# Another order of the opening table in a fused attention and MLP kernel on one core

## The chip, the core and the metric

The kernel runs on one core of a Trainium2 chip. Its engines work side by side, each on its own list of instructions in order: TensorE (PE in the profile, with the loading of weights shown apart as PEld), VectorE (DVE), ScalarE (ACT), GpSimd (POOL) and SyncE (SP). SyncE does nothing here but issue transfers. An instruction that needs another engine's result, or data from a transfer, waits on a semaphore, and everything behind it on its own engine waits with it. The metric is the device time of the whole program in microseconds; the time before is a median of 347.26 us over five runs (347.07 to 348.0).

## The reference, cut to what matters

```python
# B, H, S, D = 8, 8, 576, 64; d_model = 512, d_ff = 2048
scores = matmul(q, k.T) / sqrt(D)
cum    = cumsum(log(clip(f, 0.0001, 1.0)), axis=-1)
scores = where(causal, -1e9, scores + cum[:, :, :, None] - cum[:, :, None, :])
attn   = softmax(scores)
x      = matmul(attn, v)              # heads side by side: 4608 x 512
h      = x @ w_in                     # 4608 x 2048
out    = gelu_tanh(h) @ w_out         # 4608 x 512
```

The decay of a query divides out of the softmax. So the kernel needs only the exponentials of the scores and, for each key, a weight exp(-cum): it multiplies the values by that weight, and sums the weights themselves through the same probabilities for the denominator.

## The kernel before

The 64 pairs of batch and head are taken in 16 quads of four heads. Quad i belongs to batch i // 2. For one quad the work is as follows.

- Its keys and queries come as bf16 by GpSimd's transfers (load_one, L154) into one of two buffers each (k_c, q_c); VectorE transposes them (L160) into kT and qT.
- Scores (L215) are computed on TensorE with a key block as the stationary operand, into one of two PSUM tiles (psS), and ScalarE takes their exponential (L223) into pt. Quads 0 and 1 are cut into four rounds (split_rounds), others into three.
- Diagonal blocks of pt are masked, either on GpSimd by an affine_select (mask, L229) or on VectorE by a product with a triangle (mask_by_product, L258).
- The values of the batch, v_nat, arrive by SyncE's transfers (load_v, L131), one for each block of 128 keys. They are multiplied by the key weights into vw (make_vw, L177), on GpSimd or VectorE.
- The denominators (L269 or L283, then VectorE's L302, L304, L306) and two value products (L269 or L283, then VectorE's L314) give the quad's part of xT. Quads 0 and 1 do this in two parts, of 256 and of 320 queries; the products of the parts use one of two PSUM tiles (psM).
- When both quads of a batch are done, the MLP's input product (L325, or L342 for the first chunk of 512 tokens in halves of 256) with the GELU on ScalarE, and its output product (L363) follow. The output product is a generator, so that it is run in small pieces between other work on TensorE.

The order of the first part of the program is written out in a table, FRONT, which run() walks word by word. The scheduler is set to manual, so the place of a word in the table is the place of its instructions on each engine's list. A word is a name, its arguments, and after an @ an earlier transfer that it has to wait for (a gate). The words that the change and the prediction touch:

- LK.i, LQ.i: issue the load of quad i's keys or queries (GpSimd). LU.t: issue the load of block t of batch 0's values (SyncE). LV.b.h: the same for half the heads of batch b, five blocks. WI.c, WO.c: issue a quarter of w_in or w_out (GpSimd).
- TK.i, TQ.i: the transposes (VectorE). SB: the running sums of log f on GpSimd. CW: the key weights (TensorE, ScalarE). W: their copy as bf16 (VectorE). TR: the triangles. Z: five memsets on GpSimd.
- S.i.r: the scores of a round for four heads; H.i.r.g: for the heads of pair g alone.
- M.i.r and m.i.r: the mask on GpSimd and on VectorE. VW.i.part and vw.i.part: make_vw on GpSimd and on VectorE. CL: a small copy in vw.
- D.i.part, V.i.x.part: denominators and value products. J.half.g: a piece of the first input product. I.c.p: a piece of the second. F.c.n and f.c.n: n pieces of output product c.
- B.n.cols: n matmuls on a tile of zeros, whose result nobody reads.

GpSimd's transfers all share the software queue (q0), SyncE's the hardware queue (q1). A value block arrives in packets of 256 bytes, keys and queries in 2304 bytes, w_in in 2048, w_out in 1024.

Two gates matter most. In the table before, the load of value block 0 waits for quad 1's queries, and the first load of w_in waits for that value block:

```python
LU.1@LK.0 B.3.256                                   # SETUP
WO.0@LK.0 LU.0@LQ.1 SB TK.0 TQ.0 CW S.0.0 TR W LU.2 # FRONT, first words
WI.0@LU.0 H.1.1.0 M.1.0 D.1.0
```

After the table come the chunks 2 to 8 in a loop, which the change doesn't touch.

Of the kernel before, what the change touches and what calls it, by code (L numbers as in the profile page):

```python
# [16 lines left out]
def kernel(  # L17
# [10 lines left out]
    nc = tc.nc  # L28

    B, H, S, D = q.shape  # L30
    BH = B * H
# [35 lines left out]
    LOW, HIGH = NT, NT - 1  # L67

    SETUP = """
        LU.1@LK.0 B.3.256  # L70
    """

    FRONT = """
        WO.0@LK.0 LU.0@LQ.1 SB TK.0 TQ.0 CW S.0.0 TR W LU.2 B.2.128 B.2.384 B.4.256 Z M.0.0 TK.1 S.0.2 B.2.384 TQ.1 LU.3@LQ.1
        D.0.0 H.1.0.0 B.1.256 vw.1.0 H.1.0.1 vw.0.0 H.0.1.1 B.4.128 H.0.1.0 V.0.1.0 V.0.0.0 WI.0@LU.0 H.1.1.0 M.1.0 D.1.0 V.1.1.0 WI.1@WO.0 LU.4 m.0.1 H.0.3.1
        B.3.256 H.0.3.0 V.1.0.0 m.0.3.2 LK.3 vw.0.1 M.0.3.4 LQ.2 H.1.2.1 B.2.256 H.1.2.0 D.0.1 H.1.3.0 H.1.3.1 V.0.1.1 V.0.0.1 H.1.1.1 WI.2@LU.3 vw.1.1 m.1.1
        M.1.3 J.0.1 D.1.1 V.1.0.1 WI.3@LU.2 V.1.1.1 WO.2@LU.4 WO.1 LK.2 WO.3 LV.1.1@LK.2 J.0.0 J.1.1 TQ.2 J.1.0 J.1.2 J.0.3 J.0.2 LQ.3 LV.1.0@LK.2
        J.1.3 TK.2 F.0.6 S.2.0 LK.4 F.0.12 TQ.3 S.2.2 TK.3 F.0.10 S.2.1 TK.4 M.2.0 vw.3 M.2.2 F.0.5 F.0.5 LQ.5 S.3.0 M.2.1
        f.0.4 LQ.4 D.2 VW.2 f.0.2 LV.3.0@LK.4 CL.2 S.3.1 f.0.6 LK.5 LV.2.1@LV.3.0 V.2.0 M.3.1 S.3.2 f.0.6 TQ.4 m.3.2 CL.3 LV.2.0@LK.4 V.2.1
        S.4.1 F.0.5 H.4.2.1 M.3.0 D.3 f.0.1 H.4.0.1 H.4.0.0 LK.6 V.3.1 v.3.0 f.0.2 TQ.5 H.4.2.0 VW.5 I.1.1 I.1.6 I.1.0 LQ.7 vw.4  # L80
        I.1.2 m.4.0 TK.6 I.1.7 LQ.6 I.1.3 CL.5 I.1.5 I.1.4 F.1.8 TK.5 CL.4 LK.7 S.5.0 f.1.7 TQ.6 M.4.1 M.4.2.3 M.4.2.2 D.4
        S.5.1 LV.3.1 m.5.1 F.1.10 S.5.2 V.4.0 f.1.5 m.5.0 V.4.1 S.6.0 M.5.2 f.1.3 D.5 VW.6 f.1.4 S.6.1 V.5.1 M.6.1 f.1.5 V.5.0
        LQ.8 M.6.0 LK.8 S.6.2 CL.6 M.6.2 F.1.14
    """

    singles = ctx.enter_context(tc.tile_pool(name="singles", bufs=1))
# [6 lines left out]
    def many(n, shape, dtype, name):  # L93
        return [singles.tile(shape, dtype, name=f"{name}{i}") for i in range(n)]
# [11 lines left out]
    vw = many(2, [128, NT + 1, 4, D], BF16, "vw")  # L106
# [6 lines left out]
    logfT = singles.tile([128, NT * BH], FP32, name="logfT")  # L113
    before = singles.tile([128, (NT - 1) * BH], FP32, name="before")
# [296 lines left out]
            nc.vector.tensor_copy(m, utri_f32)  # L411
        nc.vector.tensor_copy(causal[1][64:128, 0:64], utri_f32[0:64, 0:64])

    def sums_before():
        nc.gpsimd.tensor_copy(before[:, 0:BH], logfT[:, 0:BH])
        for t in range(1, NT - 1):
            nc.gpsimd.tensor_add(before[:, t * BH:(t + 1) * BH],
                                 before[:, (t - 1) * BH:t * BH],
                                 logfT[:, t * BH:(t + 1) * BH])

# [28 lines left out]
    def load_values(b, half):  # L449
# [2 lines left out]
    ops = {  # L452
        "W": cast_w,
        "CW": make_w,
        "SB": sums_before,
        "Z": zeros,
        "TR": triangles,
        "S": lambda i, r: scores(i, r),
# [111 lines left out]
```

## Time and profile before

| quantity | value |
| --- | --- |
| median of five runs | 347.26 us |
| time of the profiled execution | 347.95 us |
| its span in the trace | 346.2 us |
| TensorE busy | 331.6 us |
| ScalarE busy | 191.1 us |
| VectorE busy | 134.9 us |
| GpSimd busy | 97.0 us |
| mean granted TensorE clock | 0.985 |

The profile is of one execution; its time is 1.7 us over its span, which lies around the recorded instructions, and 0.7 us over the median. TensorE is busy nearly throughout, so time is to be looked for in the places where it idles or where its clock is lowered. The page has the busy shares in 40 slices, and the trace answers in windows of any length, with the clock that was granted in each.

### The profile page before, as it was taken

The page shows a single profiled execution, that of the slowest core. Times are in us where ns is not written, and L with a number is a line of the kernel's source. Part 1 is how long each engine was busy: PE and PEld are TensorE (multiplying, and loading weights), DVE is VectorE, ACT ScalarE, POOL GpSimd, SP SyncE. Part 2 cuts the span into 40 slices and gives each one's busy share as a digit, 9 for nine tenths or more (in the row PEclk, how much of TensorE's full clock was granted, in tenths as well). Part 3 has the DMA queues.
Part 4 walks back from the last instruction along what each step waited for, and adds up shares of the span by engine and source line. Part 5 has one row for each costly group of instructions (what it writes and reads, how often), then busy time and mean ns, then how long its engine had stood idle before and what let it go on. Part 6 is the DMA issues. An engine that isn't in the chain of part 4 may idle for free.

```text
span 346.2 us, 9348 instructions
## 1 busy us (share of the span) xinstructions
PE 331.6 (96%) x4200; PEld 162.9 (47%) x4221; DVE 134.9 (39%) x204; ACT 191.1 (55%) x192; POOL 97.0 (28%) x139
## 2 busy tenths in 40 slices
PE   3879999999899999999999999999999999999996
PEld 2336854544454444444544444444444554444443
DVE  4766127755361534352445145404530360002011
ACT  3746577775666475746664667457655623520510
POOL 7336116233043216420552065104510320000000
PEclk9958999999999999999999999999999999999999
DMA  7998998878015871068105901380100011001002
GB/s 124 216 160 134 181 217 174 184 185 154 3 64 98 173 155 41 34 140 165 63 34 110 195 33 65 80 157 32 63 32 2 32 51 44 0 32 61 30 32 91
DMA packets 51000, 33.26 MB, mean 96 GB/s; under 512 B 38992, under 2 KB 41296, under 8 KB 50960
## 3 DMA queue, kind: packets, MB, share of 16 engines
q0 software_dynamic: 7808, 13.63, 23.8%
q1 hardware_dynamic: 43008, 18.96, 20.5%
q8 instruction: 33, 0.54, 0.7%
q10 hardware_dynamic: 144, 0.07, 0.1%
q14 instruction: 7, 0.06, 0.1%
HBM read 36.85 MB, written 9.44 MB: 134 GB/s over the span
## 4 chain that ended last, share of the span: by engine, by line
PE 90%; DMA 4%; issue 2%; POOL 2%; ACT 1%; DVE 1%; POOLq 0%; DVEq 0%; ACTq 0%
PE pso L363 35%; PE ps_h L325 32%; PE ps_s L215 9%; PE po L283 8%; PE ps_h L342 4%; DMA q_c<-in_q_dram 2%; PE po_m L269 2%; DMA v_nat<-in_v_dram 1%; ACT pt L223 1%; POOL vw L177 1%; DVE vw L177 1%; PE ps_o L283 0%; PE idle_ps L194 0%; POOL pt L229 0%; POOL k_c L154 0%
## 5 line engine op out<-in xcount | busy, mean ns | idle before, releaser
L363 PE MATMUL pso<-w_out_sb,gT 128*32 128x512 bf16 (+2 forms) x1469 | 133.9, 377 | 0.8 <-issue 0.6
L223 ACT ACTIVATE pt<-ps_s 128x1024 bf16<-128x1024 f32 (+2 forms) x100 | 94.3, 991 | 43.2 <-PE ps_s L215 41.4
L325 PE MATMUL ps_h<-xT,w_in_sb 128*128 128x512 bf16 x499 | 112.0, 379 | 0.8 <-issue 0.2
L332 ACT ACTIVATE gT<-ps_h 128x1024 bf16<-128x1024 f32 x64 | 65.5, 1023 | 77.0 <-PE ps_h L325 77.0
L363 PEld LDWEIGHTS <-gT 128*32 128x32 bf16 (+1 forms) x1477 | 56.4, 97 | 56.6 <-issue 2.4
L325 PEld LDWEIGHTS <-w_in_sb 128*128 128x128 bf16 x512 | 49.6, 98 | 61.4 <-issue 2.5
L229 POOL TENSOR_SCALAR_AFFINE_SELECT pt<-pt 128x512 bf16<-128x512 bf16 (+3 forms) x70 | 42.2, 613 | 119.4 <-ACT pt L223 114.9
L368 DVE COPY o_st<-pso 128x512 f32<-128x512 f32 (+2 forms) x37 | 25.0, 676 | 86.0 <-PE pso L363 85.9
L215 PE MATMUL ps_s<-qT,kT 32*128 32x64 bf16 (+5 forms) x896 | 38.1, 269 | 1.5 <-ACT pt L223 1.1
L302 DVE STREAM_TRANSPOSE den<-po 128x576 f32<-128x576 f32 x14 | 11.0, 783 | 53.7 <-PE po L283 53.7
L314 DVE TENSOR_TENSOR xT<-po,rb 128x576 bf16<-128x576 f32 x26 | 19.7, 757 | 29.0 <-PE po L283 28.9
L177 POOL TENSOR_TENSOR vw<-v_nat,wT 128x1280 bf16<-128x1280 f32 x12 | 28.0, 2330 | 10.7 <-DMA v_nat<-in_v_dram 10.7
L215 PEld LDWEIGHTS <-kT 32*128 32x128 bf16 x896 | 17.2, 94 | 25.5 <-issue 20.0
L160 DVE STREAM_TRANSPOSE kT<-k_c 128x576 f32<-128x576 f32 x16 | 19.9, 1246 | 10.2 <-DMA k_c<-in_k_dram 9.2
L283 PE MATMUL po<-pt,vw 128*32 128x64 bf16 (+4 forms) x624 | 22.5, 279 | 0.0
L160 DVE STREAM_TRANSPOSE qT<-q_c 128x576 f32<-128x576 f32 x16 | 19.9, 1242 | 4.7 <-DMA q_c<-in_q_dram 4.7
L154 POOL DMA_DIRECT2D k_c<-in_k_dram x16 | 9.1, 567 | 43.9 <-DVE kT L160 39.5
L283 PEld LDWEIGHTS <-vw 128*32 128x32 bf16 x672 | 14.0, 97 | 12.1 <-issue 4.7
L342 PE MATMUL ps_h<-xT,w_in_sb 128*128 128x256 bf16 x128 | 14.3, 273 | 0.0
L342 PEld LDWEIGHTS <-w_in_sb 128*128 128x128 bf16 x128 | 12.4, 98 | 1.7 <-issue 0.2
L306 DVE STREAM_TRANSPOSE rb<-rec 128x576 f32<-128x576 f32 (+2 forms) x18 | 12.8, 712 | 0.6
L283 PE MATMUL po<-pt,w_bf 128*32 128x512 bf16 (+3 forms) x336 | 12.3, 278 | 0.3 <-POOL pt L229 0.3
(59 smaller groups left out, 114.0 us busy)
## 6 DMA issues: line engine op xcount, KB each, us to landing
out_dram<-o_st SPq DMA_DIRECT2D x35, 256.0 KB, 2.1
v_nat<-in_v_dram SPq DMA_DIRECT2D x20, 256.0 KB, 6.0
k_c<-in_k_dram POOLq DMA_DIRECT2D x16, 288.0 KB, 6.0
q_c<-in_q_dram POOLq DMA_DIRECT2D x16, 288.0 KB, 6.9
v_nat<-in_v_dram SPq DMA_DIRECT2D x29, 128.0 KB, 4.4
w_out_sb<-in_moe_w_out_dram POOLq DMA_DIRECT2D x4, 512.0 KB, 10.3
w_in_sb<-in_moe_w_in_dram POOLq DMA_DIRECT2D x4, 512.0 KB, 7.0
v_nat<-in_v_dram SPq DMA_DIRECT2D x6, 64.0 KB, 4.9
```

Source lines behind the costliest of these rows:

```text
L160: nc.vector.transpose(out=dst.rearrange("p s c -> p (s c)").bitcast(FP32) .rearrange("p (t a) -> p a t", a=S // 32), in_=src.rearrange("p ...
L177: eng.tensor_mul(vw[i % 2][:, t0:t1], vb[:, t0:t1, h0:h0 + 4, :], wT[:, i, t0:t1, :].unsqueeze(3).to_broadcast([128, t1 - t0, 4, D]))
L215: nc.tensor.matmul(tiles[h // 2][:, h % 2, c0:c0 + nq], key_columns(i, key, h, c), qq[32 * h:32 * h + 32, q0:q0 + nq, c], start=(c == 0 an ...
L223: nc.scalar.activation(p[:, 2 * g:2 * g + 2, off:off + n], t[:, :, 0:n], AF.Exp, scale=scale)
L229: nc.gpsimd.affine_select(out=x, in_=x, compare_op=ALU.is_ge, fill=0.0, base=0, pattern=pattern, channel_multiplier=-1)
L283: nc.tensor.matmul(po[r0:r0 + w.shape[-1], 448 + q0:448 + q0 + nq], w, p[:, h, col:col + nq], start=(key in (0, "low")), stop=(key in ("lo ...
L314: nc.vector.tensor_mul(xT[:, 2 * u + x, S * b + s0:S * b + s1], po, rbs[i, part])
L325: nc.tensor.matmul(ph[:, j, :], w_in_sb[:, dt, 128 * ft:128 * ft + 128], xT[:, dt, CH * c:CH * (c + 1)], start=(dt == 0), stop=(dt == N_DT ...
L332: nc.scalar.activation(gT[c % 2][:, 2 * pr:2 * pr + 2, :], ph, AF.Gelu_apprx_tanh)
L342: nc.tensor.matmul(ph[:, j // 2, QA * (j % 2):QA * (j % 2) + QA], w_in_sb[:, dt, 128 * ft:128 * ft + 128], xT[:, dt, n0:n0 + QA], start=(d ...
L363: nc.tensor.matmul(pso[c0:c0 + cols, m0:m1], gT[c % 2][:, ft, 128 * n + c0:128 * n + c0 + cols], w_out_sb[:, ft, m0:m1], start=(ft == 0), ...
L368: nc.vector.tensor_copy(st[:, m0:m1], pso[:, m0:m1])
```

## The change

SETUP is emptied and FRONT gets another order. What differs, by kinds:

- Value loads. Block 4 goes first, after quad 0's keys have landed; blocks 0, 1 and 2 follow with no later gate; block 3 waits for block 4. Before, block 1 went first, block 0 waited for quad 1's queries, and 2, 3 and 4 came behind it.
- w_in and w_out. Only WI.0 keeps its gate; WI.1, WI.2 and WI.3 lose theirs, and WI.3 and WI.2 come right after the mask M.0.1. WO.0 loses its gate. WO.1 to WO.3 are issued together, WO.1 behind value block 3. Half-batch value loads LV.1.1 and LV.1.0 wait for WO.2 and LQ.3 instead of LK.2.
- The first masks of quad 1 (M.1.0) go from GpSimd to VectorE (m.1.0), as do some later ones; M.0.1 and M.1.1 go the other way. make_vw of quad 1's second part and of quads 4 and 5 is on GpSimd, of quads 2, 3 and 6 on VectorE.
- TK.1 and TQ.1 go ahead of W and TR on VectorE, both halves of quad 1's first scores go ahead of D.0.0, and D.0.0's mask M.0.0 goes ahead of the memsets Z on GpSimd.
- Zero matmuls: B.3.128 ahead of S.0.0 (768 columns become 384), 1920 columns (before: 2048) between S.0.0 and S.0.2, 1024 columns (before: 768) behind S.0.2, and one later group, B.3.256, in place of four.
- A new word, sb, would run the sums on VectorE; the table doesn't use it.

```diff
     SETUP = """
-        LU.1@LK.0 B.3.256
+        
     """
     FRONT = """
-        WO.0@LK.0 LU.0@LQ.1 SB TK.0 TQ.0 CW S.0.0 TR W LU.2 B.2.128 B.2.384 B.4.256 Z M.0.0 TK.1 S.0.2 B.2.384 TQ.1 LU.3@LQ.1
-        D.0.0 H.1.0.0 B.1.256 vw.1.0 H.1.0.1 vw.0.0 H.0.1.1 B.4.128 H.0.1.0 V.0.1.0 V.0.0.0 WI.0@LU.0 H.1.1.0 M.1.0 D.1.0 V.1.1.0 WI.1@WO.0 LU.4 m.0.1 H.0.3.1
-        B.3.256 H.0.3.0 V.1.0.0 m.0.3.2 LK.3 vw.0.1 M.0.3.4 LQ.2 H.1.2.1 B.2.256 H.1.2.0 D.0.1 H.1.3.0 H.1.3.1 V.0.1.1 V.0.0.1 H.1.1.1 WI.2@LU.3 vw.1.1 m.1.1
-        M.1.3 J.0.1 D.1.1 V.1.0.1 WI.3@LU.2 V.1.1.1 WO.2@LU.4 WO.1 LK.2 WO.3 LV.1.1@LK.2 J.0.0 J.1.1 TQ.2 J.1.0 J.1.2 J.0.3 J.0.2 LQ.3 LV.1.0@LK.2
+        TK.0 TQ.0 TK.1 B.3.128 LU.4@LK.0 WO.0 SB CW TQ.1 W S.0.0 B.1.128 TR LU.0 B.4.256 M.0.0 B.2.384 S.0.2 B.4.256 H.1.0.1
+        H.1.0.0 D.0.0 H.0.1.1 LU.1 vw.0.0 H.1.1.1 B.3.256 Z m.1.0 vw.1.0 H.0.1.0 LU.2@LK.0 WI.1 V.0.1.0 WI.0@LU.0 M.0.1 D.1.0 LU.3@LU.4 H.1.1.0 WI.3
+        WI.2 V.0.0.0 LK.2 H.0.3.1 V.1.1.0 H.0.3.0 vw.0.1 m.0.3 V.1.0.0 H.1.3.0 H.1.3.1 D.0.1 H.1.2.0 M.1.1 M.1.3 LQ.2 H.1.2.1 V.0.0.1 V.0.1.1 D.1.1
+        J.0.1 VW.1.1 V.1.1.1 WO.1@LU.3 WO.2 WO.3 LK.3 V.1.0.1 LV.1.1@WO.2 TQ.2 J.0.0 J.1.0 J.0.2 TK.2 J.1.2 J.1.1 J.0.3 J.1.3 F.0.6 LQ.3
...
-    def sums_before():
-        nc.gpsimd.tensor_copy(before[:, 0:BH], logfT[:, 0:BH])
+    def sums_before(eng):
+        eng.tensor_copy(before[:, 0:BH], logfT[:, 0:BH])
...
-        "SB": sums_before,
+        "SB": lambda: sums_before(nc.gpsimd),
+        "sb": lambda: sums_before(nc.vector),
```

The rest of the table, from S.2.0 on, is reordered too, with the same pieces of products: the output product of chunk 0 is still cut into 64 pieces in all, and that of chunk 1 into 56 within the table.

More of the change, by code (lines that the diff above doesn't have):

```diff
@@ L77 @@
-        M.1.3 J.0.1 D.1.1 V.1.0.1 WI.3@LU.2 V.1.1.1 WO.2@LU.4 WO.1 LK.2 WO.3 LV.1.1@LK.2 J.0.0 J.1.1 TQ.2 J.1.0 J.1.2 J.0.3 J.0.2 LQ.3 LV.1.0@LK.2
-        J.1.3 TK.2 F.0.6 S.2.0 LK.4 F.0.12 TQ.3 S.2.2 TK.3 F.0.10 S.2.1 TK.4 M.2.0 vw.3 M.2.2 F.0.5 F.0.5 LQ.5 S.3.0 M.2.1
-        f.0.4 LQ.4 D.2 VW.2 f.0.2 LV.3.0@LK.4 CL.2 S.3.1 f.0.6 LK.5 LV.2.1@LV.3.0 V.2.0 M.3.1 S.3.2 f.0.6 TQ.4 m.3.2 CL.3 LV.2.0@LK.4 V.2.1
-        S.4.1 F.0.5 H.4.2.1 M.3.0 D.3 f.0.1 H.4.0.1 H.4.0.0 LK.6 V.3.1 v.3.0 f.0.2 TQ.5 H.4.2.0 VW.5 I.1.1 I.1.6 I.1.0 LQ.7 vw.4
@@ L81 @@
-        I.1.2 m.4.0 TK.6 I.1.7 LQ.6 I.1.3 CL.5 I.1.5 I.1.4 F.1.8 TK.5 CL.4 LK.7 S.5.0 f.1.7 TQ.6 M.4.1 M.4.2.3 M.4.2.2 D.4
-        S.5.1 LV.3.1 m.5.1 F.1.10 S.5.2 V.4.0 f.1.5 m.5.0 V.4.1 S.6.0 M.5.2 f.1.3 D.5 VW.6 f.1.4 S.6.1 V.5.1 M.6.1 f.1.5 V.5.0
-        LQ.8 M.6.0 LK.8 S.6.2 CL.6 M.6.2 F.1.14
+        TK.0 TQ.0 TK.1 B.3.128 LU.4@LK.0 WO.0 SB CW TQ.1 W S.0.0 B.1.128 TR LU.0 B.4.256 M.0.0 B.2.384 S.0.2 B.4.256 H.1.0.1
+        H.1.0.0 D.0.0 H.0.1.1 LU.1 vw.0.0 H.1.1.1 B.3.256 Z m.1.0 vw.1.0 H.0.1.0 LU.2@LK.0 WI.1 V.0.1.0 WI.0@LU.0 M.0.1 D.1.0 LU.3@LU.4 H.1.1.0 WI.3
@@ new lines @@
+        WI.2 V.0.0.0 LK.2 H.0.3.1 V.1.1.0 H.0.3.0 vw.0.1 m.0.3 V.1.0.0 H.1.3.0 H.1.3.1 D.0.1 H.1.2.0 M.1.1 M.1.3 LQ.2 H.1.2.1 V.0.0.1 V.0.1.1 D.1.1
+        J.0.1 VW.1.1 V.1.1.1 WO.1@LU.3 WO.2 WO.3 LK.3 V.1.0.1 LV.1.1@WO.2 TQ.2 J.0.0 J.1.0 J.0.2 TK.2 J.1.2 J.1.1 J.0.3 J.1.3 F.0.6 LQ.3
+        LV.1.0@LQ.3 LK.4 S.2.0 F.0.11 S.2.2 TQ.3 F.0.10 S.2.1 m.2.0 TK.3 TK.4 vw.3 F.0.10 LV.2.0 vw.2 M.2.2 CL.3 M.2.1 S.3.0 LQ.4
+        CL.2 LQ.5 f.0.7 D.2 S.3.1 f.0.6 V.2.0 TQ.4 LK.5 S.3.2 f.0.7 m.3.0 V.2.1 S.4.1 F.0.5 H.4.2.1 M.3.1 M.3.2 D.3 H.4.0.0
@@ L84 @@
+        H.4.0.1 V.3.1 VW.4 v.3.0 LK.6 TQ.5 LV.3.0@LQ.3 f.0.2 LQ.6 H.4.2.0 TK.5 I.1.1 TK.6 LK.8 CL.4 I.1.6 LK.7 I.1.5 I.1.4 I.1.3
+        m.4.0 I.1.2 I.1.0 I.1.7 F.1.8 M.4.1 TQ.6 S.5.0 LV.2.1@LK.7 M.4.2 f.1.7 VW.5 D.4 S.5.1 F.1.6 F.1.7 S.5.2 LV.3.1 LQ.7 m.5.1
+        m.5.0 V.4.0 f.1.5 V.4.1 S.6.0 f.1.4 CL.5 vw.6 M.5.2 D.5 f.1.3 LQ.8 S.6.1 V.5.1 f.1.6 m.6.0 V.5.0 m.6.1 S.6.2 m.6.2
+        CL.6 F.1.10
     """
@@ L412, in triangles @@
         nc.vector.tensor_copy(causal[1][64:128, 0:64], utri_f32[0:64, 0:64])
-    def sums_before():
-        nc.gpsimd.tensor_copy(before[:, 0:BH], logfT[:, 0:BH])
+    def sums_before(eng):
+        eng.tensor_copy(before[:, 0:BH], logfT[:, 0:BH])
         for t in range(1, NT - 1):
-            nc.gpsimd.tensor_add(before[:, t * BH:(t + 1) * BH],
+            eng.tensor_add(before[:, t * BH:(t + 1) * BH],
                                  before[:, (t - 1) * BH:t * BH],
```

## The prediction, written before the changed kernel was run

> **What bounds it now.** I read the page's busy rows first, then the trace in windows, then the chain of waits, then the transfers.
>
> ```profile
> PE 331.6 (96%) x4200; PEld 162.9 (47%) x4221; DVE 134.9 (39%) x204; ACT 191.1 (55%) x192; POOL 97.0 (28%) x139
> ...
> PEclk9958999999999999999999999999999999999999
> ```
>
> TensorE is the bound, and its work is the same after the change but for zero matmuls. So time can come only from its idle time, or from a slice with a low clock; the row has one, the third (17 to 26 us). Windows over the front show both (columns: window, then us, then busy us and count of PE, PEld, DVE, ACT, POOL, then granted clock, DMA share, GB/s):
>
> ```profile
> 12.10:16.60 4.50, 4.02 (x57) 1.97 (x55) 2.28 (x5) 3.65 (x6) 1.29 (x3) 1.00 1.13 223
> 16.60:19.10 2.50, 0.04 (x2) 0.00 (x0) 2.47 (x2) 1.12 (x2) 2.49 (x4) 0.94 0.94 168
> 19.10:29.00 9.90, 9.87 (x131) 4.19 (x133) 5.74 (x13) 4.85 (x7) 2.45 (x5) 0.50 0.97 153
> 29.00:34.00 5.00, 4.89 (x116) 3.62 (x104) 3.45 (x7) 4.05 (x5) 4.20 (x6) 1.00 0.78 133
> 34.00:46.20 12.20, 12.20 (x120) 10.91 (x113) 2.86 (x5) 6.14 (x6) 1.52 (x3) 1.00 1.15 187
> ```
>
> TensorE stands for 2.5 us and then runs 9.9 us at half clock. The chain of waits says what the 2.5 us are:
>
> ```profile
> 3.52 7.90 DMA q_c<-in_q_dram
> ...
> 11.44 4.80 DMA v_nat<-in_v_dram
> ...
> 16.94 2.14 DVE vw L177
> ...
> 19.13 0.83 PE po_m L269 x16
> ```
>
> Quad 1's queries land at 11.4; only then is value block 0 issued (its gate), and it lands at 16.24; then VectorE makes vw. The timeline shows that of two equal products the second took three times as long, beside two GpSimd masks:
>
> ```profile
> 16.33 0.69 DVE L177 TENSOR_TENSOR vw<-v_nat,wT 128x512 bf16<-128x512 f32 x1 [1.35 <-DMA v_nat<-in_v_dram]
> 16.94 2.13 DVE L177 TENSOR_TENSOR vw<-v_nat,wT 128x512 bf16<-128x512 f32 x1
> 17.29 1.23 POOL L229 TENSOR_SCALAR_AFFINE_SELECT pt<-pt 128x512 bf16<-128x512 bf16 x2
> ```
>
> **The change, part by part.**
>
> *Start to 14 us.* SB, CW, TK.0, TQ.0 and S.0.0 hang on loads that stay where they are: S.0.0 starts at 9.75 again, its exponentials end at 12.12, M.0.0 (1.23) ends at 13.5. The zero matmuls beside it cost nothing while S.0.2 waits for a PSUM tile. TK.1 and TQ.1 now stand ahead of W; quad 1's queries land at 11.4, so TQ.1 ends at 11.45 + 1.24 = 12.7, W (0.33 + 0.19) at 13.3, TR at 13.8.
>
> *D.0.0 later.* Both halves of quad 1's first scores now precede it. They wait for the PSUM tiles of S.0.2, freed by exponentials at 13.3 and 14.0. D.0.0 runs at 14.4 instead of 13.0, and VectorE's 0.45 + 0.20 + 0.45 behind it end at 16.15 (before 15.0). This is a loss of 1.15 us on VectorE, hidden because it waited for values until 16.33 anyway.
>
> *The values.* vw.0.0 needs blocks 0 and 1. Now the queue is 4, 0, 1, 2 (128 + 3x256 KB, issued from 5.6 to 7.9), with 3 after block 4. What they get depends on the software queue. The queue rows of two windows, 11.0 to 13.5 (w_out running) and 14.0 to 15.5 (software queue empty); columns packets, MB, share:
>
> ```profile
> q0 software_dynamic: 426, 0.43, 102.1%
> q1 hardware_dynamic: 312, 0.08, 21.0%
> ```
>
> ```profile
> q1 hardware_dynamic: 1489, 0.37, 115.0%
> q0 software_dynamic: 7, 0.00, 1.8%
> ```
>
> Alone the values get 0.37/1.5 = 250 GB/s, beside w_out 0.08/2.5 = 32. Before, the hardware queue had moved about 0.31 MB by 14.0 (I summed its packets by half microseconds), all in gaps of the software queue. With the same gaps blocks 4, 0, 1 (0.66 MB) are in 0.35/0.25 = 1.4 us later, 15.4, landed about 15.7. So vw.0.0 starts at 16.15: no gain yet.
>
> *The mask off GpSimd.* vw.0.0 takes 0.69, m.1.0 two products of 0.42, vw.1.0 0.69; GpSimd issues WI then and masks nothing. V.0.1.0 needs vw.0.0 alone. The Trainium skill ("SBUF — State Buffer", section on two separate sides) says that VectorE with two SBUF inputs and GpSimd lock each other out for whole instructions, whichever **starts first**. The row shows the lock (2.13 against 0.69), not that order: the product is recorded 0.35 us ahead of the mask and still lost. By the rule GpSimd would have lost, and moving the mask gain nothing; by the row it gains 1.44. I take the row.
>
> *TensorE from 15 us.* H.0.1.1, H.1.1.1, zeros, H.0.1.0 follow each other as exponentials (1.02 each from 15.6) free the tiles, then V.0.1.0 at 17.35 against 19.13. The idle gap is gone.
>
> *The clock.* By "TensorE: Matmul & The Clock Gate" (its goals table) gaps under about 3 us don't drop the clock; this trace dropped it at 18.9 after 2.5 us idle. By the rule the half clock isn't the gap's doing and would stay; by the row it goes with the gap. I take the row: it starts at the gap's end.
>
> *17.35 to J.0.0, at full clock.* ScalarE then sets the pace: exponentials to 18.7 and 19.75, four of 0.81 to 23.0. VectorE: xT, D.1.0's three, two xT to 20.85, vw.0.1 (1.16) to 22.0, m.0.3 to 22.7. D.0.1 (0.70 for its 20 matmuls) 22.7 to 23.3; H.1.2 to 24.0; V.0.0.1 and V.0.1.1 (0.75 each) to 25.6; D.1.1 26.2; J.0.1 (1.92) 28.1; V.1.1.1 and V.1.0.1 29.6. Before, J's long run began at 34.04. **Gain 4.4 us.** VW.1.1 on GpSimd is between 1.1 (VectorE's 0.69 to 1.16 rows scaled) and 1.4 (2.33 x 768/1280); at 26.3 it is 1.8 us early.
>
> *w_in.* WI.1 is issued at 15.3 behind Z (1.83), WI.0 at 16.0; at 150 GB/s their 1.05 MB are in by 24, needed at 26.2. WI.3 and WI.2, behind M.0.1 (18.7 to 19.4), land by 30.2; J.0.2 needs them at 33.1. Keys and queries of quad 2 land by 33.6, WO.1 to WO.3 at 200 GB/s by 41.4; J ends near 41.8 and F.0.11 comes at 44. The transfers stay 1 to 3 us ahead: GpSimd's stalls at its gates (3.0 us before WI.0, DMA share 0.31 to 0.61 near 26 and 32) no longer empty the queue. The new gate WO.1@LU.3 stands behind VW.1.1, which needs block 3 itself: nothing. WO.0, issued a microsecond sooner, still queues behind quad 1's loads: nothing. LK.4 waits on TK.2, and behind it on GpSimd stand masks of quad 2 that come ten microseconds later.
>
> *Value blocks 2 and 3 against w_in.* Block 3 is last in its queue. From 14.0 to 16.8, when WI.1's packets begin (1.5 us after issue, as WI.0's did), 0.7 MB pass; 0.15 MB, some 600 packets, are left to share with w_in. At 98 packets in half a microsecond (when WI.0 met values at 18.0) they end at 20; at the 312 per 2.5 us above, at 21.6. vw.0.1 wants them at 20.85. I charge **0.5 us**, with one collision of vw.0.1 with M.1.1 (0.61) partly in it.
>
> *After 42 us.* Batch 1's values wait at new gates: LV.1.1 for WO.2 (38.8), LV.1.0 for LQ.3 (45). Beside the software queue they crawl until it empties near 47; 1.2 MB at 250 GB/s then end at 52. vw.3 (before 55.6, now 51.3) and vw.2 can hold VectorE up to 1 us; V.2.0, the first to need them, comes at 57. Masks and vw swap engines: vw.2 and vw.6 cost VectorE 1.48 each and free GpSimd of 2.33 each, vw.4 goes the other way. VectorE is 13.4 of 20 us busy at 60 to 80, so they fit. TensorE idles 0.3, 1.1 and 0.2 us in 60:80, 80:100 and 100:120; the 1.1 is S.5.1 behind a table load, with the same f.1.7 ahead. Zero, between -0.5 and +1.0.
>
> *Sum.* 4.4 - 0.5 = 3.9. The profiled execution would go from 347.95 to 344.05; it lay 0.7 over the median, so **343.4 us** for the median.
>
> **Rivals.**
>
> *The clock drops all the same (0.18).* Between 19 and 22.3 TensorE has only scores of two heads and short value products; it was busy all through 19 to 29 before and the clock stayed low. If another such stretch halves it, 1.8 us (17.35 for 19.13) remains, with 1.4 us of zero matmuls saved there (0.82 + 0.61 in the timeline) less the 0.5 and some collisions: gain 2, 345.3 us. Against it: 12.1 to 16.6, as sparse, kept full clock.
>
> *Value block 3 starves behind w_in: slower (0.14).* "DMA: Bandwidth & Descriptors" (Arbitration) has the queues take turns by packets; block 1 took 9.7 us to land behind the software queue. If 900 packets are still to come and get 80 a microsecond, block 3 lands at 28. vw.0.1 then holds VectorE, behind it m.0.3, D.0.1 and the xT: +7.2 on a gain of 4.4, so about 350.1. It decides from a landing of 25.3 on. Against: 0.7 MB pass alone first.
>
> *The two cancel (0.06).* Block 3 lands near 25: 347.3. No difference that can be told, which for this kernel is within 0.2%, 0.7 us.
>
> **How the numbers follow.** The forecast has 0.62. Faster: 0.62 + 0.18 = 0.80; same 0.06; slower 0.14. Its own range is 342.0 (nothing charged, 0.5 found later) to 344.9 (1.5 lost to arrivals or later order); the clock's rival reaches 346.5. So 342.0 to 346.5.
>
> **What would show it.** No TensorE gap over 1 us between 14 and 30; clock 1.00 from 12 on; the first vw at 0.7 us; J's run starting near 29.6; everything from 110 on shifted whole. A VectorE wait on v_nat at vw.0.1 of over 1 us, or a clock of 0.5 near 20, would prove me wrong, as would a wait on w_out at F.0.11.

## The result, and the profile after

The ratio of the changed kernel's time to the time before is 0.9919, with a 95% interval of 0.9901 to 0.9938: 0.8% faster, which on the shown median of 347.26 us is 344.4, against 343.4 forecast. It rests on the executions that are within 1.5% of each kernel's fastest, and that is 11 of the changed kernel's 36; taken over all 36 its times run from 342.57 to 356.05 us with a median of 350.41, where 71 executions of the kernel before have a median of 347.89 and go no higher than 349.57. So the gain is there when the order works, and in most executions it is more than lost: 23 of the 36 are above the longest of the kernel before. The question of this study is what decides between the two.

The profiled execution is one of the long ones: 354.24 us, span 352.5, clock 0.976. The changed kernel's other profile, in experiment 12, is of a long execution too; no short one was profiled. The busy row and clock row on the page of the first:

```profile
PE 330.9 (94%) x4200; PEld 163.1 (46%) x4221; DVE 136.9 (39%) x209; ACT 190.9 (54%) x192; POOL 92.1 (26%) x131
...
PEclk9965999999999999999999999999999999999999
```

TensorE works as long as before (330.9 against 331.6 us) and the lowered clock now spans two slices. The windows of the changed kernel's front (columns: window, us, then busy us and count of PE, PEld, DVE, ACT, POOL, then granted clock, DMA share, GB/s):

```profile
12.10:16.60 4.50, 4.32 (x55) 2.32 (x53) 3.03 (x9) 4.45 (x6) 3.65 (x8) 1.00 1.28 231
16.60:19.10 2.50, 1.45 (x26) 0.78 (x25) 2.25 (x4) 1.19 (x3) 1.17 (x2) 1.00 1.14 190
19.10:24.50 5.40, 4.83 (x64) 1.99 (x64) 2.22 (x7) 3.81 (x5) 2.19 (x4) 0.54 1.04 184
24.50:33.10 8.60, 0.00 (x0) 0.00 (x0) 2.58 (x3) 0.33 (x1) 4.06 (x5) 0.50 0.94 177
33.10:40.10 7.00, 6.96 (x136) 4.47 (x135) 4.38 (x11) 3.60 (x4) 3.06 (x5) 0.75 0.90 139
40.10:52.30 12.20, 12.20 (x120) 10.93 (x113) 2.84 (x4) 6.14 (x6) 0.54 (x1) 1.00 1.11 213
```

The gap of 16.6 to 19.1 is partly filled (1.45 us of 2.5 busy, before 0.04), but behind it a new one of 8.6 us has opened, from 24.5 to 33.1, and the clock is at half from 19.5 to 36.6: 17.1 us, before 10.2. J's long run starts at 40.11 against 34.04 before. Its 12.2 us after that are as busy as they were. The list of waits between 10 and 60 us names the gap's owner (columns: engine, operation and tile, what it waited for, then us in all, times, longest):

```profile
DVE vw L177 <- DMA v_nat<-in_v_dram: 10.1, 2, 8.7
...
PE po_m L269 <- DVE pt L258: 8.7, 1, 8.7
...
POOL vw L177 <- DMA v_nat<-in_v_dram: 4.1, 1, 4.1
```

VectorE's timeline puts a time on it (start, duration, then in brackets the idle time before it and its releaser):

```profile
16.85 0.69 DVE L177 TENSOR_TENSOR vw<-v_nat,wT 128x512 bf16<-128x512 f32 x1 [1.41 <-DMA v_nat<-in_v_dram]
...
18.12 1.12 DVE L177 TENSOR_TENSOR vw<-v_nat,wT 128x512 bf16<-128x512 f32 x1
...
30.52 0.96 DVE L177 TENSOR_TENSOR vw<-v_nat,wT 128x768 bf16<-128x768 f32 x1 [8.70 <-DMA v_nat<-in_v_dram]
```

The two first products take 0.69 and 1.12 (before 0.69 and 2.13): the masks are off GpSimd there. But vw.0.1, which needs value blocks 2 and 3, waits 8.7 us for the values, and behind it on VectorE stand the mask m.0.3, then D.0.1 on TensorE and everything up to J. What the queues did in the last 8.3 of these microseconds, 22.0 to 30.3 (packets, MB, share):

```profile
q0 software_dynamic: 868, 1.70, 108.5%
q1 hardware_dynamic: 147, 0.04, 3.1%
```

The last 147 packets of block 3, 256 bytes each, took 8.3 us beside 868 packets of the software queue, that is of w_in, keys and queries. The load itself, issued at 14.60:

```profile
v_nat<-in_v_dram SPq DMA_DIRECT2D x1, 256.0 KB, 15.8
```

SyncE's timeline shows why it was issued so late (start, duration; first the issue of block 2, then that of block 3):

```profile
10.46 3.59 SPq L131 DMA_DIRECT2D v_nat<-in_v_dram  x1
...
14.60 0.59 SPq L131 DMA_DIRECT2D v_nat<-in_v_dram  x1
```

Issuing block 2 alone held SyncE for 3.59 us, to 14.05, at a time when the values hardly moved (243 packets of the hardware queue from 8 to 12 us). Only the 0.5 us after that are the gate: block 4 landed at 14.6 (issued at 5.59, 9.0 us). The load of block 3 then took 15.8 us where block 0 took 4.8 in the kernel before.

That all of it is in the front shows in one window of each kernel over the unchanged rest, first before, then changed:

```profile
106.00:346.20 240.20, 236.00 (x2886) 111.06 (x2898) 77.44 (x108) 123.94 (x122) 55.77 (x71) 1.00 0.30 73
```

```profile
112.40:352.50 240.10, 235.49 (x2884) 110.79 (x2896) 78.82 (x111) 124.33 (x122) 54.59 (x68) 1.00 0.29 71
```

240.2 against 240.1 us, at full clock in both. The profiled span is 6.3 us longer; J's long run starts 6.1 later. The executions of the changed kernel also sort by clock: 342.6 and 342.9 us at 1.00, 344.0 to 344.3 at 0.99, 344.8 to 346.6 at 0.983 to 0.985, 348 to 351 at 0.98, and 350 to 356 from 0.976 down.

### The profile page after: what moved, and what is told of

The parts are those of the page before. It is cut to its first block, busy times and chain, and to the rows that moved or that the text cites. A ratio compares the mean times of both kernels' runs of the same rounds, so it can differ in the third digit from the quotient of the medians.

```text
span 352.5 us, 9344 instructions
## 1 busy us (share of the span) xinstructions
PE 330.9 (94%) x4200; PEld 163.1 (46%) x4221; DVE 136.9 (39%) x209; ACT 190.9 (54%) x192; POOL 92.1 (26%) x131
## 4 chain that ended last, share of the span: by engine, by line
PE 80%; POOL 1%; issue 1%; ACT 1%; POOLq 0%; DVE 0%
PE pso L363 33%; PE ps_h L325 31%; PE po L283 8%; PE ps_s L215 7%; POOL vw L177 1%; ACT pt L223 1%; PE ps_o L283 0%; POOL pt L229 0%; POOLq L566 0%; DVE o_st L368 0%; POOLq L229 0%
## 5 line engine op out<-in xcount | busy, mean ns | idle before, releaser
L332 ACT ACTIVATE gT<-ps_h 128x1024 bf16<-128x1024 f32 x64 | 65.5, 1024 | 76.1 <-PE ps_h L325 76.1
L229 POOL TENSOR_SCALAR_AFFINE_SELECT pt<-pt 128x512 bf16<-128x512 bf16 (+3 forms) x62 | 37.3, 613 | 124.7 <-ACT pt L223 123.4
L177 POOL TENSOR_TENSOR vw<-v_nat,wT 128x1280 bf16<-128x1280 f32 (+1 forms) x12 | 27.9, 2324 | 13.9 <-DMA v_nat<-in_v_dram 13.9
L160 DVE STREAM_TRANSPOSE kT<-k_c 128x576 f32<-128x576 f32 x16 | 19.9, 1244 | 3.1 <-DMA k_c<-in_k_dram 1.8
L160 DVE STREAM_TRANSPOSE qT<-q_c 128x576 f32<-128x576 f32 x16 | 19.9, 1244 | 0.3 <-DMA q_c<-in_q_dram 0.2
L342 PE MATMUL ps_h<-xT,w_in_sb 128*128 128x256 bf16 x128 | 14.3, 273 | 0.0
L349 ACT ACTIVATE gT<-ps_h 128x1024 bf16<-128x1024 f32 x8 | 8.2, 1024 | 8.3 <-PE ps_h L342 8.3
```

The lines of the kernel that those rows point to most:

```text
L160: nc.vector.transpose(out=dst.rearrange("p s c -> p (s c)").bitcast(FP32) .rearrange("p (t a) -> p a t", a=S // 32), in_=src.rearrange("p ...
L177: eng.tensor_mul(vw[i % 2][:, t0:t1], vb[:, t0:t1, h0:h0 + 4, :], wT[:, i, t0:t1, :].unsqueeze(3).to_broadcast([128, t1 - t0, 4, D]))
L229: nc.gpsimd.affine_select(out=x, in_=x, compare_op=ALU.is_ge, fill=0.0, base=0, pattern=pattern, channel_multiplier=-1)
L332: nc.scalar.activation(gT[c % 2][:, 2 * pr:2 * pr + 2, :], ph, AF.Gelu_apprx_tanh)
L342: nc.tensor.matmul(ph[:, j // 2, QA * (j % 2):QA * (j % 2) + QA], w_in_sb[:, dt, 128 * ft:128 * ft + 128], xT[:, dt, n0:n0 + QA], start=(d ...
```

## The experiments

The theory after the result was that the forecast order works where value block 3 arrives by about 21 us, and that otherwise VectorE waits for it behind w_in. The rivals were: the gate of block 3 alone is at fault; the removed gates on w_in are at fault; the clock is lost in any case. Each kernel below was timed beside the kernel before, in the same session on the same chip; times are the median and range of all its executions, and the ratio is built as in the section above.

**1. w_in behind block 3.** In the changed kernel, block 3's issue is moved up and the first w_in quarter is gated on it.

```diff
- LU.2@LK.0 WI.1 V.0.1.0 WI.0@LU.0 M.0.1 D.1.0 LU.3@LU.4 H.1.1.0
+ LU.2@LK.0 LU.3@LU.4 WI.1@LU.3 V.0.1.0 WI.0@LU.0 M.0.1 D.1.0 H.1.1.0
```

> The changed kernel, but the first w_in load (WI.1) waits for value block 3, whose word moves ahead of it; SyncE's order is the same. Theory (block 3's last packets starve beside w_in on the software queue): block 3 lands near 18 to 19 us, VectorE waits for values at vw.0.1 under 1 us (8.7 us in the profile of the changed kernel), and all executions lie in 342.5 to 347 us, median 344.5. Rival (the late executions come from the clock, halved by sparse TensorE work near 20 us, and the wait for values is only beside it): the spread from 343 to 356 us stays, median 350.

Measured: 347.46 us (345.06 to 349.68, 12 executions), the kernel before 347.54; ratio 1.0001 (0.9966 to 1.0036), not the 344.5 expected. In its profile (347.48 us, clock 0.995) vw.0.1 no longer waits and runs at 20.25, and D.1.1 is done near 25.3. The waits of 10 to 60 us then name w_in:

```profile
POOL w_in_sb L143 <- DMA v_nat<-in_v_dram: 3.7, 1, 3.7
...
PE ps_h L342 <- DMA w_in_sb<-in_moe_w_in_dram: 3.4, 1, 3.4
```

GpSimd stands 3.7 us at the new gate, and J.0.1, which could have run at 25.3, stands 3.4 us for w_in until 28.7. So block 3's wait is the cause of the executions over 350 (none is left), but the gain was not to be had this way: in this front either the values or w_in are late. Something else has to leave it.

**2. Block 3 without its gate.** The changed kernel with `LU.3@LU.4` written as `LU.3`.

> The changed kernel without the gate of block 3 on block 4, so that it is issued near 8 us and not at 14.6. Theory (w_in is what starves block 3, the gate only adds to it): less of block 3 is left when w_in starts, median 346 to 348 us, but single executions over 350 us remain. Rival (the gate alone makes block 3 late): it lands by 18 us in all executions, median 344, none over 347. If neither the gate nor w_in mattered: 350 us as before.

Measured: 348.41 us (344.72 to 352.87, 12), before 347.54; ratio 0.998 (0.9933 to 1.0028). Four of twelve are still at 351.7 to 352.9, so the gate alone is not the cause. How much it adds this run can't say, since it hardly moves the issue that the expectation put near 8 us. In its profile SyncE is held at block 2 as before, to 14.3, and then issues block 3:

```profile
14.36 1.08 SPq L131 DMA_DIRECT2D v_nat<-in_v_dram  x1
```

That is 0.24 us sooner than with the gate. vw.0.1 waits 2.86 us for the values there and runs at 24.49.

**3. The removed gates alone.** The kernel before, with two gates taken off.

```diff
- WI.0@LU.0 H.1.1.0 M.1.0 D.1.0 V.1.1.0 WI.1@WO.0
+ WI.0 H.1.1.0 M.1.0 D.1.0 V.1.1.0 WI.1
```

> The kernel before with the gates of WI.0 and WI.1 taken away and nothing else: w_in's packets start near 15 us, 3 us sooner, while blocks 0, 2, 3 and 4 are still on their way. Starvation theory: the value products come later, median 350 us or more and a spread of 5 us or more. Rival (the queues share evenly, the gates cost GpSimd 3.0 us for nothing): 345 to 348 us with the narrow spread of before.

Measured: 346.48 us (343.41 to 347.22, 12), before 347.54; ratio 0.9954 (0.9929 to 0.998). My expectation of over 350 failed and the rival's held. Two quarters of w_in issued early don't starve the values here. GpSimd, no longer held at the gate, starts the mask at 15.20 instead of 17.29, so that less of it meets the two products: 1.73 us for the pair instead of 2.74. The removed gates are not the fault as such.

**4. The mask alone.** The kernel before, with `M.1.0` written as `m.1.0`.

> The kernel before with one edit: quad 1's first mask on VectorE (m.1.0), so that GpSimd masks nothing beside the value products. If the two engines locked each other out: both products of 512 columns take 0.69 us, the TensorE gap of 2.5 us shrinks to about 1.1, gain 1.4 us (346.4), and up to 5 us if the clock then stays full. Rival (the long product has another cause): one still takes 2.1 us and the time stays within 347 to 348.5.

Measured: 346.25 us (342.17 to 346.80, 12), before 347.54; ratio 0.9936 (0.9903 to 0.9969). From the timeline of a profile at 342.63 us:

```profile
15.63 1.29 DVE L177 TENSOR_TENSOR vw<-v_nat,wT 128x512 bf16<-128x512 f32 x2 [0.52 <-DMA v_nat<-in_v_dram]
```

The pair takes 1.29 instead of 2.74 us: that is the lock, priced as the prediction had it (1.44). The times fall in groups by the clock of the record: three at 342.2 to 342.8 with 1.00, one at 344.9 with 0.99, eight at 346.2 to 346.8 with 0.985. So removing the lock is worth 1.3 us, and the clock, where it then holds, another 3.7.

**5. The gap filled, nothing else.** The kernel before with eleven zero matmuls in front of the waiting V.0.1.0.

```diff
- H.0.1.0 V.0.1.0 V.0.0.0
+ H.0.1.0 B.11.512 V.0.1.0 V.0.0.0
```

> The kernel before with 11 zero matmuls of 512 columns (2.35 us at full clock) set into TensorE's 2.5 us gap ahead of the first value product, nothing else. If the gap is what halves the clock: clock 0.995 to 1.0 in most executions, median 344 us, as the kernel before's own executions at clock 1.0 take (344.05, 344.65). Rival (the sparse score and value products after the gap halve it): clock 0.985 and 347.5 us as before.

Measured: 344.80 us (344.25 to 345.33, 6), before 348.14; ratio 0.9907 (0.9881 to 0.9933); clock 1.00 in all six. The window that stood idle in the kernel before, and the first half of the one at half clock:

```profile
16.60:19.10 2.50, 2.50 (x23) 1.13 (x25) 2.18 (x2) 0.93 (x2) 2.49 (x5) 1.00 0.97 162
19.10:24.00 4.90, 4.90 (x105) 2.45 (x97) 4.31 (x10) 3.89 (x5) 1.61 (x4) 1.00 1.04 156
```

The pair of value products still takes 2.74 us; the zeros only keep TensorE busy through the gap. That alone is worth 3.3 us, so in this order the half clock was the gap's doing, and not that of the sparse products behind it. Experiment 7 shows that this is not the whole rule.

**6. The first quarter of w_out out of the way.** Experiment 1 said that the front has too much to carry. WO.0 is 512 KB that F.0.6 first needs at 46.3 us in the kernel before and at 52.3 in the changed one's profile, and it is the first thing on the software queue after quad 1's loads. In the changed kernel it is moved to the other quarters of w_out.

```diff
- LU.4@LK.0 WO.0 SB CW
+ LU.4@LK.0 SB CW
...
- WO.1@LU.3 WO.2 WO.3
+ WO.0 WO.1@LU.3 WO.2 WO.3
```

> The changed kernel with one load moved: the first quarter of w_out (WO.0) goes from ahead of the values to just ahead of WO.1. Theory (the front is short of transfers: what goes ahead of values and w_in makes one of them late, whatever the gates): 3 us of the software queue are freed, all value blocks land by 17 us, w_in by 26, median 343 us, none over 346. Rival (the load is only paid later, F.0.6 waits for it near 42): median 346 to 347. If block 3 is late for its gate alone: 350 as for the changed kernel.

Measured: 341.50 us (341.37 to 342.00, 6), before 348.14; **ratio 0.9814 (0.9787 to 0.9841)**. It beats both kernels, and its executions lie within 0.63 us, where the changed kernel's are spread over 13.5. The queues between 9.5 and 14.4 us:

```profile
q1 hardware_dynamic: 4056, 1.02, 122.8%
q0 software_dynamic: 36, 0.06, 6.4%
```

1.02 MB of values pass before w_in begins, at about 210 GB/s (1.02 MB in 4.9 us). All three products on VectorE are then at their plain price and none waits for values:

```profile
15.34 0.65 DVE L177 TENSOR_TENSOR vw<-v_nat,wT 128x512 bf16<-128x512 f32 x1
...
16.58 0.69 DVE L177 TENSOR_TENSOR vw<-v_nat,wT 128x512 bf16<-128x512 f32 x1
...
19.23 0.94 DVE L177 TENSOR_TENSOR vw<-v_nat,wT 128x768 bf16<-128x768 f32 x1
```

The windows show the front as it was forecast for the changed kernel, some 2 us earlier still:

```profile
16.60:19.10 2.50, 2.45 (x56) 1.37 (x56) 2.43 (x8) 2.50 (x4) 1.21 (x2) 1.00 1.01 139
19.10:24.00 4.90, 3.84 (x100) 2.23 (x100) 4.73 (x10) 4.10 (x7) 4.40 (x8) 1.00 1.05 174
24.00:29.00 5.00, 5.00 (x90) 4.00 (x83) 2.47 (x6) 1.92 (x2) 4.14 (x6) 1.00 1.12 211
```

V.0.1.0 runs at 16.53, J.0.1 at 24.52, J's long run at 27.53. The w_out quarters, issued from 24.55 on, land 10.0 to 15.4 us later; the first output product runs at 39.8 and waits for none of them.

**7. The same without block 3's gate** (`LU.3` for `LU.3@LU.4` in kernel 6).

> As the run with WO.0 moved, and block 3 without its gate on block 4. Theory: block 3 is in before w_in starts in every execution; median 342.5 to 343.5 us with a spread under 3 us. Rival (the gate doesn't matter once WO.0 is away): the same time as with the gate, within 0.5 us.

Measured: 341.50 us (341.32 to 342.95, 6), before 348.14; ratio 0.982 (0.9793 to 0.9847). With WO.0 away the gate decides nothing. Its profile (341.99 us) has the clock at half for 3.4 us all the same, though TensorE had not stood for more than 0.2 us at a time in the 7 us before:

```profile
16.00:20.50 4.50, 4.12 (x88) 2.16 (x88) 4.43 (x11) 4.39 (x6) 3.03 (x5) 1.00 0.96 131
20.50:23.80 3.30, 3.27 (x58) 1.51 (x60) 2.53 (x7) 2.13 (x4) 2.70 (x5) 0.50 1.11 202
```

Kernel 6's profile passes the same work at full clock. What besides a gap drops the clock stays open.

**8. Mask and WO.0 in the order before.** The kernel before with the edit of 4, and WO.0 moved behind the front; WI.1, which was gated on WO.0, loses its gate.

```diff
- WO.0@LK.0 LU.0@LQ.1 SB
+ LU.0@LQ.1 SB
...
- H.1.1.0 M.1.0 D.1.0 V.1.1.0 WI.1@WO.0
+ H.1.1.0 m.1.0 D.1.0 V.1.1.0 WI.1
...
- WO.2@LU.4 WO.1 LK.2 WO.3
+ WO.0 WO.2@LU.4 WO.1 LK.2 WO.3
```

> The kernel before with two edits: quad 1's first mask on VectorE (alone: 346.25 us) and WO.0 moved to just ahead of the other w_out loads. Theory: value blocks 1 and 0 land near 14.5 instead of 16.2, TensorE has no gap, the clock stays full in most executions, 342 to 344 us. Rival: 346, the mask's gain alone, because WO.0 is missed later.

Measured: 345.45 us (343.76 to 346.09, 6), before 348.14; ratio 0.992 (0.989 to 0.9949), not the 342 to 344 expected, and with three of six at a clock of 0.985. In its profile (344.69 us, full clock) the front is as early as kernel 6's (J.0.1 at 23.57, J at 27.66), and then TensorE waits twice:

```profile
34.13 6.94 PE L342 MATMUL ps_h<-xT,w_in_sb 128*128 128x256 bf16 x62 [0.84 <-DMA w_in_sb<-in_moe_w_in_dram]
...
44.46 0.69 PE L215 MATMUL ps_s<-qT,kT 32*128 32x64 bf16 x24 [2.09 <-DVE kT L160]
```

0.84 us are for w_in, whose last quarter is issued at 25.0 here, and at 18.5 to 19.9 in kernel 6: a part of what the change brings lies there. The 2.09 for quad 2's keys are, as far as the profile shows, of the edit's own making: it puts a third quarter of w_out ahead of them, and they land 15.2 us after their issue where they took 11.9 in the kernel before. WO.0 behind those keys, in the order before, was not tried.

**9. Only the third issued quarter of w_in held back.** The changed kernel with `WI.3` written as `WI.3@LU.3`.

> The changed kernel with one gate: the third w_in load issued (WI.3) waits for value block 3, so that at most two quarters of w_in stream while block 3 is on its way. If the unbroken stream of w_in, keys and queries is what holds up block 3's last packets: block 3 lands by 24 us in every execution, 344 to 348 us, none over 350. Rival (block 3 is late already from its gate and the first two quarters): executions over 350 us stay, median 350.

Measured: 347.10 us (343.82 to 349.38, 12), before 347.82; ratio 0.9956 (0.9929 to 0.9984). No execution is over 350. So the first two quarters of w_in don't starve block 3; the unbroken row of WI.3, WI.2 and quad 2's keys behind them does. In its profile vw.0.1 runs at 21.17 without a wait, but the first product waited 1.30 us for values, to 16.28, and the clock is 0.51 already from 16.6 on. That is the group at 0.985.

**10. The mask back on GpSimd in kernel 6.**

```diff
- Z m.1.0 vw.1.0
+ Z vw.1.0
...
- WI.0@LU.0 M.0.1 D.1.0
+ WI.0@LU.0 M.1.0 M.0.1 D.1.0
```

> The version with WO.0 moved (341.5 us), with quad 1's first mask back on GpSimd behind the two w_in loads and so beside the value products. If the lock costs here as in the kernel before: a value product of 2 us, a TensorE gap of 1 to 2 us, 342.7 to 343.5 us, more where the clock drops. Rival (VectorE saves the mask's own 0.75 us, which pays for the lock): 341.5 within 0.5.

Measured: 343.98 us (341.57 to 344.62, 6), before 347.82; ratio 0.9877 (0.985 to 0.9904), clock at 0.984 to 0.990 in five of six. From the timeline of the profile (344.62 us):

```profile
15.12 2.15 DVE L177 TENSOR_TENSOR vw<-v_nat,wT 128x512 bf16<-128x512 f32 x2
...
16.08 2.28 POOL L229 TENSOR_SCALAR_AFFINE_SELECT pt<-pt 128x512 bf16<-128x512 bf16 x3
...
17.82 0.28 PE L269 MATMUL po_m<-pt,w_bf 128*1 128x128 bf16 x4 [0.75 <-POOL pt L229]
```

The pair of products takes 2.15 us beside the masks, against 1.34 (0.65 + 0.69) without them; D.1.0 waits 0.75 us for the mask, and the clock goes. Beside kernel 6's median, from another session, the mask's place is worth 2.5 us (2.2 by the two ratios). But the one execution at full clock took 341.57, as kernel 6 does. So most of what is lost seems to go with the clock and not with the lock itself; that execution has no profile that would show its products.

**11. Only WO.0 moved, in the order before** (the edit of 8 without its m.1.0, so WI.1 loses its gate here too).

> The kernel before with WO.0 moved to just ahead of the other w_out loads and nothing else. Theory (transfers in front decide): values land 1.3 to 1.8 us sooner, the gap before the first value product keeps its mask collision; 345.5 to 346.5 us. Rival (w_in and quad 2's keys then come no sooner, and take the gain back): 347 to 348.

Measured: 345.00 us (343.84 to 348.17, 7), before 347.82; ratio 0.9923 (0.9891 to 0.9954), within the error of 8. The collision with the mask that was expected to stay is gone: the values come before the mask, and the pair takes 1.25 us, as in 8. So neither 8 nor 11 says anything of the mask's place. One move of one transfer brings the order before nearly as far as the whole reordering brought it at its best; the waits for w_in (1.20) and for quad 2's keys (2.08) follow as in 8.

**12. The changed kernel again**, nothing edited, in another session.

> The changed kernel itself once more, on the chip of the runs with one gate and with WO.0 moved: its spread is expected again, 343 to 356 us with a median near 350, since what holds up block 3 differs from execution to execution. Rival (the spread belonged to the chip of the first comparison): a narrow spread near 344.

Measured: 352.65 us (344.55 to 355.83, 12), before 347.82; ratio 0.9982 (0.9941 to 1.0023). Nine of twelve are over 350. In the profile (354.74 us) vw.0.1 waits 8.2 us for values, until 30.1. The spread belongs to the order, not to one session.

## Why the prediction was right, and where it was not

**The direction and the size hold where the values come in time.** 344.4 us was measured on the compared executions against 343.4, inside 342.0 to 346.5. That it lies so near is in part luck. Only two of the 36 executions show the full clock that the forecast rests on, at 342.6 and 342.9; the other nine compared lowered it, at 344.0 to 346.6, and the mixture makes 344.4. Over all 36 the median is 350.4, slower than before. By the prediction's own signs the profiled execution proves it wrong: vw.0.1 waits 8.7 us for values, and the clock is at half from 19.5. Its mechanisms were each seen at work, though most of them in kernels other than the changed one:

- *The gap.* V.0.1.0 was forecast at 17.35 (before 19.13); it ran at 17.59 in the profile. But TensorE still stood for 0.96 us ahead of it, where the prediction has no gap.
- *The lock.* The prediction took the row against the order that the Trainium skill gives ("SBUF — State Buffer", two separate sides). The runs agree with the row: the pair takes 1.29 us without the mask in experiment 4, and 2.15 beside it in 10.
- *The clock.* It took the row again, against the 3 us of "TensorE: Matmul & The Clock Gate". Experiment 5 shows it: filling a gap of 2.5 us kept the clock and saved 3.3 us. That the half clock starts at the gap's end is not so: it started at 18.8, inside the gap.
- *The undisturbed order.* J.0.1 was forecast at 26.2 and J's run at 29.6; in kernel 6, where nothing comes late, they ran at 24.5 and 27.5. That run gains 6.5 us on J's start (34.04 to 27.53) and 6.6 on the median, so the rule that the time follows J's start was sound. The engines' part of the sum was 2 us too cautious; 0.9 of these stand at the start, since S.0.0 was taken over at 9.75 and ran at 8.82 (8.84 in the changed kernel's profile).
- *The rest.* No loss after 42 us: the two windows over the rest are equal, and nothing waits for w_out.

**The step that failed is "value blocks 2 and 3 against w_in", charged with 0.5 us.** In the profile it costs the 8.7 us that vw.0.1 waits (it ran at 30.5 against 20.85). Four terms in it were off:

- *The issue.* The sum puts block 3 last in its queue and has no term for the time of its issue. It was issued at 14.60, since SyncE stood for 3.59 us at block 2, and its last packets met w_in. In kernel 6 it was issued at 11.84.
- *What is left.* I had some 600 packets left at 16.8; at 17.0 there were 1050 (903 up to 22.0, and the last 147).
- *The rate.* The 98 packets in half a microsecond are misread: the kernel before moved 80 in 18.0 to 18.5, and 98 in the whole of 18 to 19. Up to 22 us the changed kernel's values ran at 181 a microsecond (903 in 5 us), near the rates I used, so they would have been in at 22.8, 2 us late. What I had no term for is the tail: 147 in 8.3 us, 18 a microsecond. With turns taken by packets ("DMA: Bandwidth & Descriptors", Arbitration), and if the page's packets are those of the trace, 868 software packets over 16 engines are 54 for each engine, an estimate from the queue rows; 147 value packets taken in turn with them would be done after some 10 of the 54 if they were spread over all engines. They took the whole time, which would fit packets that are left on only two or three of the engines (147/54 = 2.7). The trace has no row by engine, so this stays an inference.
- *WO.0.* I left it at "nothing", since it queues behind quad 1's loads. It fills the queue from about 10 to 14 us, the only time in which the values could have passed alone: in kernel 6 they do, and without that 0.5 MB the time falls to 341.5 and the spread is gone.

**The chance of the rival was the larger error.** "Value block 3 starves" had 0.14, with a landing at 28 and 350.1 us. In the two profiles vw.0.1 ran at 30.1 and 30.5, and 20 of 36 executions are over 350. It named the mechanism, but I set its chance by the one arrival I had worked out, not by how near the two streams ran: block 3's last packets were to end at 20 to 21.6 with 20.85 the limit and one more unbroken stream beside them. The rival of the clock (0.18, 345.3) is what six of the eleven compared executions look like: 0.983 to 0.985 at 344.8 to 346.6. Its cause is only in part known. In the profile the clock falls at 19.5, behind the first product's wait for block 1 (landed at 16.7 against the 15.7 forecast), which leaves a part of the old gap standing; experiment 9's profile shows that pair, wait and clock, together, and no run took the wait away without taking more. The sparse stretch of 19 to 22 us that the rival named is not cleared: kernel 6's profile passes it at full clock with 3.84 of 4.9 us busy, kernel 7's loses the clock in it.

Three small terms: vw.1.0 took 1.12 us beside the mask M.0.1, where 0.69 was written; make_vw on GpSimd took 1.49 us in kernel 6 where 1.1 to 1.4 was given. And the range's low end, 342.0, is 0.4 under what its two terms make of 343.4 (0.5 not charged and 0.5 found: 342.4).

## What to carry to other kernels

Order the transfers of all queues by the time they are needed before tuning any gate: one 512 KB load that was due some 20 us after the values made either the values or the weights late. Moving it was worth some 9 us of the median in the changed order, and 2.8 in the order before, with one gate fewer. Give a queue of small packets its time alone: here its tail beside an unbroken stream of large packets ran at 18 packets a microsecond, against some 830 nearly alone. Look at how long the issuing engine is held, too, before blaming a gate. Where two streams end within a microsecond of each other, look at the spread of many executions, not at the best or at one profile. Fill a short wait of TensorE with matmuls on zeros where the clock record shows a drop in it or behind it.

## What the runs showed of the hardware that was not expected

- A TensorE gap of 2.5 us went with a halved clock from 18.8 to 29.0; eleven zero matmuls in the gap kept it at 1.00 in six of six executions and saved 3.3 us.
- The idle time of TensorE alone doesn't tell when the clock falls. It fell after 0.7, 0.3 and 0.6 us of it in the 3.4 us before (profiles of experiments 2, 7 and 9), and stayed full with up to 0.9, 0.8 and 1.2 us of it in such a stretch (6, 8 and 11).
- In the nine profiles in which the clock fell it was at half for 3.4 us (experiments 1 and 7), 10.2 (the kernel before, 2, 3, 9 and 10), 17.1 (the changed kernel) or 20.5 (12): whole multiples of about 3.4 us.
- 147 packets of 256 bytes took 8.3 us beside 868 of the software queue (1.70 MB), while 4056 of them passed in 4.9 us nearly alone.
- A single issue of a value load held SyncE for 3.59 us while the hardware queue hardly moved, and with it every load behind.
- The same program, in one session on one chip, took from 344.6 to 355.8 us (experiment 12); with the one load moved, 341.4 to 342.0 in another session. That two queues' sharing of the DMA engines makes the difference fits both profiles of long executions, in which vw.0.1 waits over 8 us for values.
- A VectorE product that is recorded as starting ahead of a GpSimd mask was still the one that was held (16.94 against 17.29 in the kernel before, 2.13 us); in experiment 10 the second product of the pair, at 15.88 ahead of a mask at 16.08, took 1.40.
